# Seven gated sums of an S2-MLP block: from VectorE and GpSimd to GpSimd alone

## The chip, the cores and the metric

The kernel runs on one core of one Trainium2 chip. The core has a matrix engine (TensorE, PE in the profile; its weight loads are PEld), a vector engine (VectorE, DVE), an engine for functions and copies (ScalarE, ACT), a general engine (GpSimd, POOL), and SyncE (SP), which here issues most of the DMAs. Each engine works through its own list of instructions in the order in which the program was written, and waits on semaphores for the others. The metric is the device time of one execution, in microseconds (us); lower is better.

## What is computed

A block with adaptive layer norm: attention with 32 heads over 2048 tokens of width 512, and then a mixer in two halves, each part gated by a row made from the condition c.

```python
h = _layernorm(x, axis=-1) * (1 + ca) + sa
x = x + ga * _A_ref(h, A_wqkv, A_wo)            # attention
h = _layernorm(x, axis=-1) * (1 + cb) + sb
x = x + gb * _B_ref(h, B_w1, B_w2, B_w3, B_w4)  # the mixer

# _B_ref(x):
h = _gelu(_layernorm(x, axis=-1) @ w1)
hs = shifted(h) @ w2          # four quarters of the columns, shifted by +1, -1, +2, -2 rows
x1 = x + hs                   # the mixer's first half
h2 = _gelu(_layernorm(x1, axis=-1) @ w3) @ w4
return x1 + h2
```

Seen from the result, the mixer adds gb * x1 and gb * h2 to x. The change concerns the first of these two sums.

## The kernel before

**Tiles and chunks.** The 2048 rows are 16 tiles of 128 rows (NKT = 16); four tiles are a chunk (TPC = 4, NC = 4). Attention takes the first three quarters of the time. Its softmax works on all engines, and GpSimd prepares the low parts of the probabilities (L1061). What comes after attention is the tail: for every chunk wo, a layer norm, w1 with gelu, the shift and w2, a layer norm, w3 with gelu, and w4. Chunk 0's tail begins while attention still runs.

**Precision.** Each matmul of the tail is three matmuls in a reduced format, of high and low parts (`mm3`, L358 to 364: lines 359, 361 and 363). So each operand is split: ScalarE copies the high part, VectorE or GpSimd subtracts for the low one. For an activation transposed on TensorE that is L353 and L349, both into A; for a gelu's result it is L1459 and, on GpSimd, L1460. Weights of w3 and w4 are split at their first use (`fresh`, L1191): a load to `raw`, for w4 alone a GpSimd multiplication by the gate's row gbrow (L1210), ScalarE's copy (L1211), VectorE's subtraction (L1212), and then a store to Ws in DRAM for later chunks, from which the rings of weights are loaded.

**One tile in the tail.** `tail(ci)` (L1283) is a generator of chunk ci's work up to w2. Here x1 is the tile of x and xb the tile of the mixer. After wo, VectorE adds the result to x1 (`x1_add`, L1406), takes statistics (L370, L371, L1353), GpSimd makes the reciprocal root (`rstd`, L1356), and VectorE writes the modulated norm to xb (`center` L1415, `scale` L1418). A second norm follows: statistics of xb, GpSimd's `shift` (L1356, L1360 and L1361, three operations on the small tile trs), and ScalarE's xn (`ln_apply`, L1367). TensorE transposes xn (L1247), and w1 follows. After w2, VectorE adds its result to xb (`xb_add`, L1511), and the same statistics, shift and xn (L370, L1356, L1367) make w3's input. Then xb holds half of the mixer's first half (gelu's factor of one half is left out on the way), and the list `z` (L1515, L1516) adds it to x1 with the gate: VectorE multiplies xb by 2 and by gbrow, and GpSimd adds xb to x1. `rest(ci)` (L1527) does w3 and w4 and adds w4's result to x1 (`z_add`, L1560); the tile is then stored (L1568).

Chunk 0 takes tiles 0, 1, 2 through w2 (the shift wants the rows after a tile). Chunk 1 takes tiles 3 and 4, then 5 and 6; chunk 2 takes 7 to 10, and chunk 3 takes 11 to 15.

**The order of the work.** `Sched` (L112) plans the order of each engine's instructions while the program is written; nothing is decided on the chip. It keeps a planned time for PE, ACT, DVE and POOL (T["P"], "A", "D", "G"). A generator's matmuls advance PE's time. Operations that follow are put into a chain, a list of (engine, cost, function); the next one is ready 170 ns after the one before (XX). `misc` (L171) picks from the chains the operation for an engine that can start first, and, among equals, the one of the chain that stands first in the list, by its priority (`prio`: 1 for the norms, and 2, the last, for z, ZPRIO at L75) and then by age. It takes an operation only if it fits:

```python
if start + ch[1][0][1] <= until + AGE * max(0.0, self.T[e] - ch[0]) and (not best or start < best[0]):
```

Here start is the later of the engine's time and the time when the operation is ready, ch[1][0][1] is its cost, ch[0] the time when it is ready, and AGE is 0.2. In the tail, `step` (L295) sets the horizon `until` 500 ns beyond the later of the engine's time and PE's time + 100 ns. The costs are `cD` = 602 ns and `cG` = 2.2 x 512 + 40 = 1166 ns for a tile of 512 columns; a `shift` counts 850 ns and a `rstd` 464 (L1364, L1363). The `rstd` of `center` is put into GpSimd's list at once (L1414).

`mark(("z", t))` notes that tile t's sum has been put into the lists. Only then does `rest` put w4's matmuls for that tile (L1554), and `tail(ci)` of chunks 2 and 3 begins its tile t only when tile t - 8 has that mark (L1399).

Of the kernel before, what the change touches and what calls it, by code (L numbers as in the profile page):

```python
# [15 lines left out]
OP = mybir.AluOpType  # L16
# [4 lines left out]
S, D, H, DH, F = 2048, 512, 32, 16, 1792  # L21
# [5 lines left out]
TPC = CH // P  # L27
# [294 lines left out]
def cD(n=CH):  # L322
    return n / 0.96 + 69


def cG(n=CH):
    return 2.2 * n + 40
# [3 lines left out]
def kernel(ctx, tc, A_x, A_wqkv, A_wo, B_w1, B_w2, B_w3, B_w4, c, w_mod, out):  # L331
    nc = tc.nc
    te, act, dve, pool, dma = nc.tensor, nc.scalar, nc.vector, nc.gpsimd, nc.sync
# [21 lines left out]
    def mark(key):  # L355
        return None, 0, lambda: done.add(key)
# [44 lines left out]
    gbrow = con.tile([P, D], F32, name="gbrow")  # L401
# [23 lines left out]
    def dbank(n):  # L425
        return sch.take(lambda i: psd["d"].tile([P, CH], F32, name=n, tag=f"s{i}" if psd["s"] else f"d{i}", bufs=1))
# [308 lines left out]
    for i in range(NV):  # L735
        t = qp.tile([P, H // 4, 192], BF16, name=f"vt{i}")
# [486 lines left out]
    def pool_of(ci):  # L1223
        return fa if ci < NB or (ci - NB) % 2 else tp
# [28 lines left out]
    def spawn(gen, key):  # L1253

        def run():
            yield from gen
            done.add(key)
        sch.add(run(), 0)

    def rows_mm(b, lhs, w, ks, nk):  # L1260

        for k in ks:
            wh, wl = w[k // 2]
            for _ in mm3(b, lhs(k, 0), lhs(k, 1), wh[:, k % 2], wl[:, k % 2], k == 0, k == nk - 1):
                yield nsq(CH)
# [17 lines left out]
    def tail(ci):  # L1283
# [56 lines left out]
        else:  # L1340
            t = oh[0].tile([P, NRAW, CH], F32, name="raw", tag="osb0", bufs=1)
# [3 lines left out]
        def ln_ops(src, mean=False):  # L1345

            st = fa.tile([P, 6], F32, name="tst", tag="tst", bufs=8)
            mv = fa.tile([P, 2], F32, name="tmv", tag="tmv", bufs=10)
            rs = fa.tile([P, 2], F32, name="trs", tag="trs", bufs=10)

            def stats():
                ln_stats(st, mv, src)
                dve.tensor_scalar(mv[:, 1:2], mv[:, 1:2], EPS, None, op0=OP.add)  # L1353

            def rstd():
                pool.tensor_tensor(rs[:, 0:1], mv[:, 1:2], mhalf[:, 0:1], op=OP.pow)  # L1356

            def shift():
                rstd()
                pool.tensor_tensor(rs[:, 1:2], mv[:, 0:1], rs[:, 0:1], op=OP.mult)  # L1360
                pool.tensor_scalar(rs[:, 1:2], rs[:, 1:2], -1.0, 1.0, op0=OP.mult, op1=OP.mult)  # L1361
            if mean:
                return rs, mv, (("D", cD() + 150, stats), ("G", 464, rstd))  # L1363
            return rs, (("D", cD() + 150, stats), ("G", 850, shift))  # L1364
# [10 lines left out]
        def normed(key, t, rs):  # L1375
            tag = xtag(key, t)
            xlive[tag] = xlive.get(tag, 0) + 1
            x = xn[key, t] = (tp if tag == "x4" else fa).tile([P, D], F32, name="xn", tag=tag, bufs=XN[tag])
            y = xbt[t]
            return ln_apply(x, y, rs), mark((key, t))  # L1380
# [6 lines left out]
        def xn_room(key, t):  # L1387
            return xlive.get(xtag(key, t), 0) < XN[xtag(key, t)]

        def norm_T(ts, key, i):  # L1390

            yield lambda: all((key, t) in done for t in ts) and (key == "xn" or not ci or ("w3", ci - 1) in done)
            An[key, i] = A = tA("A4" if key == "xn4" else "A", i, len(ts) * P)
            yield from transposed(lambda k, j: xn[key, ts[j]][:, k * P:(k + 1) * P], range(KT), len(ts), A)
            xlive[xtag(key, ts[0])] -= len(ts)

        for i, t in enumerate(new):
# [4 lines left out]
            x1 = x1t[t]  # L1402
            xb = xbt[t] = pool_of(ci).tile([P, D], F32, name="xb", tag="xb", bufs=XBF if pool_of(ci) is fa else XBT)
# [98 lines left out]
        for si, ts in enumerate(sub):  # L1502
            yield lambda: all(("g", ci, i, n) in done for i in range(1 + (t0 + 1 in ts)) for n in range(4))
            for t in ts:
                yield lambda: sch.room() and xn_room("xn4", t)
                b = dbank("w2")
                yield from rows_mm(b, lambda k, p: g[:, k, p, 130 + (t - t0) * P - SH[k]:][:, :P], w, range(KT), KT)
                xb, x1 = xbt[t], x1t[t]

                def xb_add(xb=xb, b=b):  # L1510
                    dve.tensor_tensor(xb, xb, b, op=OP.add)  # L1511
                    sch.free(b)

                r, ops = ln_ops(xb)
                z = (("D", cD(), lambda xb=xb: dve.scalar_tensor_tensor(xb, xb, 2.0, gbrow, op0=OP.mult, op1=OP.mult)),  # L1515
                     ("G", cG(), lambda xb=xb, x1=x1: pool.tensor_tensor(x1, x1, xb, op=OP.add)), mark(("z", t)))  # L1516
                sch.chain(("D", cD(), xb_add), *ops, *normed("xn4", t, r),
                          (None, 0, lambda z=z: sch.chain(*z, prio=ZPRIO)), bank=b, prio=NPRIO)
            spawn(norm_T(ts, "xn4", si), ("T4", ci, si))
# [82 lines left out]
    for k, blk in enumerate(blocks + [[]] * (LAG + CPER)):  # L1602
# [18 lines left out]
        t, start = CIN, 0.0  # L1621
# [53 lines left out]
        if blk and blk[0] <= 2 * (NS - T0S) <= blk[-1]:  # L1675
            sch.add(tail(0))
# [9 lines left out]
    with ExitStack() as ex:  # L1686
        ep = ex.enter_context(tc.tile_pool(name="ep", bufs=1, space=PSUM))
        psd["d"], psd["s"] = ep, False
        att.close()
        akx.close()  # L1690
        tpx = ExitStack()
        tp = tpx.enter_context(tc.tile_pool(name="tp", bufs=1))
        big["A"] = tp.tile([P, 4 * KT * 2 * P], F32R, name="A")
        big["g2"] = tp.tile([P, 4 * KT * 2 * P], F32R, name="g2")
        done.add("C")
        rings["f"] = Ring(FRONT * (NC - NB), [("wf", BF)] * BF)
        for ci in range(NB, NC):
            sch.add(tail(ci), ci - NB)
        while sch.busy():
            sch.step()  # L1700
        tpx.close()
# [29 lines left out]
```

## Time and profile before

| what | us |
|---|---|
| time, median of 3 runs | 2021.24 |
| lowest and highest | 2019.19, 2022.35 |
| profiled execution | 2021.44 |
| its span, first to last instruction | 2019.7 |
| TensorE busy | 1934.4 |
| VectorE busy | 1656.3 |
| GpSimd busy | 1571.9 |
| ScalarE busy | 1510.2 |

The views shown below are read so. A row of the page names a group of instructions by its line, engine and operation, with out<-in by the program's names. In a stretch of time the columns are the busy times of PE, PEld, DVE, ACT and POOL with the number of instructions in brackets, the granted clock of TensorE as a part of full speed, the busy share of the DMA engines, and GB/s. A list of waits gives engine and line, whom it waited for, the us in total, how often, and the longest. A row of the timeline gives the start and the duration in us, the engine, the line, the operation with its shapes, and in square brackets how long the engine stood idle just before, and who ended that. Merged rows (x2 and more) count several instructions in a row.

### The profile page before, as it was taken

To read this page: it belongs to the slowest core of one execution; us is meant where nothing else is said; L and a number is where in the kernel's file an instruction comes from. 1 tells how busy PE (TensorE), PEld (TensorE's weight loads), DVE (VectorE), ACT (ScalarE), POOL (GpSimd) and SP (SyncE) were. 2 spreads that over 40 slices of the span, in tenths; PEclk is the share of its full clock that TensorE was granted. 3 is DMA by queue.
4 is the path that set the end of the run, shared out by engine and by line. 5 is a ranking of instruction groups with operands and counts; after the bars stand their busy time and mean duration, and the time that the engine had idled before them with its cause. 6 is when DMAs were issued, how large, how long until landed. Compare 5 with 4: busy or idle time off the path is not lost.

```text
span 2019.7 us, 41655 instructions
## 1 busy us (share of the span) xinstructions
PE 1934.4 (96%) x14456; PEld 1162.1 (58%) x14456; DVE 1656.3 (82%) x2979; ACT 1510.2 (75%) x3085; POOL 1571.9 (78%) x1488
## 2 busy tenths in 40 slices
PE   7999999999999999999999999999998999999999
PEld 5755545454444444444444444444455878898998
DVE  6398888879999999999999999999975886556443
ACT  6438987768999999999999999999985544344443
POOL 6349988879999999999999999999996554435222
PEclk9989999999999999999999999999999999999999
DMA  8777675445343434444443435354414676553541
GB/s 295 233 204 192 151 187 155 135 130 124 86 92 87 91 88 83 96 82 97 81 98 75 104 72 107 72 136 126 99 46 158 230 261 265 226 200 116 201 153 68
DMA packets 185508, 278.01 MB, mean 138 GB/s; under 512 B 117104, under 2 KB 127856, under 8 KB 169008
## 3 DMA queue, kind: packets, MB, share of 16 engines
q1 hardware_dynamic: 181792, 267.20, 49.1%
q10 hardware_dynamic: 2304, 4.20, 0.6%
q0 software_dynamic: 1200, 3.93, 0.5%
q8 instruction: 115, 1.88, 0.4%
q14 instruction: 97, 0.79, 0.1%
HBM read 211.81 MB, written 62.91 MB: 136 GB/s over the span
## 4 chain that ended last, share of the span: by engine, by line
PE 61%; DVE 16%; ACT 9%; issue 6%; POOL 4%; DMA 3%; SPq 0%; ACTq 0%; POOLq 0%; DVEq 0%
PE mb L996 13%; DVE mx L992 12%; PE pv L1086 9%; PE sc L1012 8%; ACT pt L1008 7%; PE w L363 5%; PE w L359 5%; PE w L361 5%; PE pv L1083 4%; PE ot L1113 3%; POOL pt L1061 2%; PE xT L1247 1%; POOL trs L1356 1%; PE v L359 1%; DMA wr<-Ws 1%
## 5 line engine op out<-in xcount | busy, mean ns | idle before, releaser
L1061 POOL TENSOR_SCALAR pt<-pt 128x1024 f16<-128x1024 uint16 x953 | 1248.3, 1367 | 79.9 <-ACT pt L1008 76.7
L992 DVE TENSOR_REDUCE mx<-mb 128x1 f32<-128x512 f32 x2048 | 1250.0, 681 | 72.7 <-PE mb L996 63.5
L1008 ACT ACTIVATE pt<-sc 128x512 int32<-128x512 f32 x2048 | 1060.9, 614 | 123.5 <-PE mb L996 97.1
L996 PE MATMUL mb<-kst,qtl 62*128 62x512 f32 x2048 | 781.1, 461 | 20.5 <-ACT pt L1008 10.0
L1012 PE MATMUL sc<-qtl,kst 64*128 64x512 f32 x2048 | 739.3, 449 | 4.6 <-DVE mx L992 1.8
L996 PEld LDWEIGHTS mb<-kst,qtl 62*128 62x128 f32 x2048 | 358.9, 193 | 233.7 <-ACT pt L1008 160.4
L1012 PEld LDWEIGHTS sc<-qtl,kst 64*128 64x128 f32 x2048 | 336.6, 185 | 185.4 <-DVE mx L992 118.7
L1086 PE MATMUL pv<-pt,vst 128*32 128x512 f16 x4096 | 384.8, 397 | 20.6 <-ACT ac L1103 20.6
L1460 POOL TENSOR_TENSOR g<-sq,g 128x256 fp32r<-128x256 f32 (+1 forms) x124 | 96.8, 785 | 188.9 <-ACT g L1459 176.6
L1083 PE MATMUL pv<-pt,vst 128*32 128x512 f16 (+1 forms) x2048 | 220.8, 389 | 2.5 <-POOL pt L1061 2.4
L1086 PEld LDWEIGHTS <-vst 128*32 128x32 bf16 x4096 | 91.8, 93 | 227.2 <-issue 208.8
L361 PE MATMUL w<-A,wr 128*128 128x256 f32 (+1 forms) x520 | 153.4, 295 | 0.3 <-DVE A L349 0.3
L359 PE MATMUL w<-A,wr 128*128 128x256 f32 (+1 forms) x520 | 153.2, 295 | 0.3 <-ACT A L353 0.3
L363 PE MATMUL w<-A,wr 128*128 128x256 f32 (+1 forms) x520 | 153.1, 294 | 0.0
L1456 ACT ACTIVATE sq<-w 128x256 f32<-128x256 f32 (+1 forms) x130 | 52.1, 401 | 127.0 <-PE w L363 117.5
L363 PE MATMUL w<-wr,g 128*128 128x512 f32 x270 | 106.5, 394 | 3.1 <-POOL g L1460 3.1
L359 PE MATMUL w<-wr,g 128*128 128x512 f32 x270 | 106.9, 396 | 1.8 <-DMA wr<-Ws 1.8
L361 PE MATMUL w<-wr,g 128*128 128x512 f32 x270 | 106.1, 393 | 0.0
L1438 DVE SCALAR_TENSOR_TENSOR sq<-sq,w 128x256 f32<-128x256 f32 (+1 forms) x130 | 58.1, 449 | 56.5 <-ACT sq L1458 56.3
L359 PEld LDWEIGHTS w<-A,wr 128*128 128x128 f32 x520 | 98.7, 190 | 1.7 <-ACT A L353 0.5
L361 PEld LDWEIGHTS w<-A,wr 128*128 128x128 f32 x520 | 98.7, 190 | 1.6 <-DVE A L349 0.5
L363 PEld LDWEIGHTS w<-A,wr 128*128 128x128 f32 x520 | 98.6, 190 | 0.5 <-issue 0.5
(156 smaller groups left out, 2131.6 us busy)
## 6 DMA issues: line engine op xcount, KB each, us to landing
wr<-Ws SPq DMA_DIRECT2D x66, 1024.0 KB, 5.2
vst<-Vs SPq DMA_DIRECT2D x64, 768.0 KB, 5.7
kst<-Ks SPq DMA_DIRECT2D x126, 384.0 KB, 6.1
Ws<-wr SPq DMA_DIRECT2D x14, 1024.0 KB, 5.0
qtl<-Qs SPq DMA_DIRECT2D x128, 96.0 KB, 4.3
Vs<-vt SPq DMA_DIRECT2D x32, 384.0 KB, 4.2
Ks<-qk SPq DMA_DIRECT2D x16, 512.0 KB, 3.8
Qs<-qk SPq DMA_DIRECT2D x16, 512.0 KB, 3.0
```

The lines of the kernel that those rows point to most:

```text
L359: te.matmul(o, lh, rh, start=first, stop=False)
L361: te.matmul(o, lh, rl, start=False, stop=False)
L363: te.matmul(o, ll, rh, start=False, stop=last)
L992: end = sch.crit("D", 605, e + PX, lambda: dve.reduce_max(mxs[u][:, j, g, c:c + 1], b, axis=AX.X))
L996: return ready, lambda: te.matmul(b, lhs, kst[u % 3][r, c * CH:(c + 1) * CH], start=True, stop=True), after
L1008: ea = sch.crit("A", 480, e + PX, lambda: act.activation(pt[s][:, j], b, AF.Exp))
L1012: return ready, lambda: te.matmul(b, kst[u % 3][r, kt * P:(kt + 1) * P], qst[u][r], start=True, stop=True), after
L1061: e_low[s] = XP["G"] + sch.crit("G", 1345, ready, lambda: pool.tensor_scalar(o, i, 0.5, 1.0, op0=OP.mult, op1=OP.mult))
L1083: te.matmul(acc[r:r + n, :], v[:, kt + i, c:c + n].bitcast(F16), pt[s + i].bitcast(F16)[:, j, 0::2], start=False, stop=kt == NKT - 2, skip ...
L1086: te.matmul(acc[r:r + 32, :], v[:, kt, r:r + 32], pt[s].bitcast(F16)[:, j, 1::2], start=kt == 0, stop=False, skip_group_check=True)
L1113: te.matmul(b[:, t * n:(t + 1) * n], ac[:, t * P:(t + 1) * P], smat.rearrange("p j d -> p (j d)"), start=True, stop=True)
L1460: ("G", cG(n), lambda: pool.tensor_tensor(lo, sq, hi, op=OP.subtract)), (None, 0, end), bank=b)
```

## The change

For the tiles t below 2 * TPC - 1 = 7, which are those that chunks 0 and 1 take through w2, the two operations of z become one GpSimd step with a planned cost of three times cG. In it GpSimd multiplies xb by gbrow and then adds xb to x1 twice, in place of VectorE's multiplication by 2 and gbrow and GpSimd's one addition. Tiles 7 to 15 keep the list that they had. The mark, the priority and the place of the chain after xn are the same.

```diff
                 r, ops = ln_ops(xb)
-                z = (("D", cD(), lambda xb=xb: dve.scalar_tensor_tensor(xb, xb, 2.0, gbrow, op0=OP.mult, op1=OP.mult)),
+                def z_sum(xb=xb, x1=x1):
+                    pool.tensor_tensor(xb, xb, gbrow, op=OP.mult)
+                    pool.tensor_tensor(x1, x1, xb, op=OP.add)
+                    pool.tensor_tensor(x1, x1, xb, op=OP.add)
+
+                z = (("G", 3 * cG(), z_sum), mark(("z", t))) if t < 2 * TPC - 1 else \
+                    (("D", cD(), lambda xb=xb: dve.scalar_tensor_tensor(xb, xb, 2.0, gbrow, op0=OP.mult, op1=OP.mult)),
                      ("G", cG(), lambda xb=xb, x1=x1: pool.tensor_tensor(x1, x1, xb, op=OP.add)), mark(("z", t)))
                 sch.chain(("D", cD(), xb_add), *ops, *normed("xn4", t, r),
                           (None, 0, lambda z=z: sch.chain(*z, prio=ZPRIO)), bank=b, prio=NPRIO)
```

## The prediction

> **What bounds the kernel now.** I first read the page's busy shares, then the busy time in stretches, to find the stage that holds the changed operations.
>
> ```profile
> span 2019.7 us, 41655 instructions
> PE 1934.4 (96%) x14456; PEld 1162.1 (58%) x14456; DVE 1656.3 (82%) x2979; ACT 1510.2 (75%) x3085; POOL 1571.9 (78%) x1488
> ```
>
> The profiled execution took 2021.44 us: the span and 1.74 us around it. It stands 0.20 us above the median of the three runs, 2021.24. TensorE (PE) is busy 96% of the span, so a change pays or costs only where PE stands still. Next, the two edited lines and three stretches of 40 us around them.
>
> ```profile
> L1515 DVE SCALAR_TENSOR_TENSOR xb<-xb,gbrow x16: 675/682/918, 1558.7 to 1864.8; 128x512 f32<-128x512 f32 x16
> L1516 POOL TENSOR_TENSOR x<-x,xb x16: 1268/1292/1717, 1559.7 to 1865.6; 128x512 f32<-128x512 f32 x16
> ...
> 1560.00:1600.00 40.00, 34.91 (x170) 31.06 (x171) 34.47 (x65) 17.90 (x34) 23.67 (x30) 0.91 0.56 196
> 1600.00:1640.00 40.00, 36.55 (x220) 32.41 (x220) 31.20 (x62) 22.03 (x49) 23.27 (x34) 1.00 0.78 280
> 1640.00:1680.00 40.00, 36.38 (x188) 31.93 (x187) 35.70 (x64) 20.97 (x42) 24.28 (x24) 1.00 0.75 273
> ...
> 1720.00:1760.00 40.00, 40.00 (x229) 34.93 (x229) 25.66 (x55) 14.51 (x34) 18.27 (x29) 1.00 0.56 212
> ```
>
> The columns are PE, weight loads, VectorE (DVE), ScalarE (ACT), GpSimd (POOL), granted clock, DMA share and GB/s. All sixteen gated sums lie between 1558 and 1866 us; the seven that change lie before 1640. There PE loses 12.16 us in 120 (40 minus 34.91, 36.55 and 36.38), while from 1720 to 1760 it loses none. DVE is the fullest helper, 34.47 and 35.70 of 40; POOL has some 16 us free in each stretch. Then I listed what PE waited for from 1540 to 1720, and where.
>
> ```profile
> PE xT L1247 <- ACT xn L1367: 12.6, 7, 2.9
> PE w L363 <- POOL g L1460: 2.2, 1, 2.2
> ...
> 1563.87 2.40 PE L1247 MATMUL xT<-ident,xn 128*128 128x128 f32 x10 [2.94 <-ACT xn L1367]
> 1582.53 0.98 PE L1247 MATMUL xT<-ident,xn 128*128 128x128 f32 x7 [1.54 <-ACT xn L1367]
> 1605.38 0.98 PE L1247 MATMUL xT<-ident,xn 128*128 128x128 f32 x7 [2.52 <-ACT xn L1367]
> 1652.70 0.50 PE L363 MATMUL w<-wr,g 128*128 128x512 f32 x1 [2.23 <-POOL g L1460]
> 1659.21 0.98 PE L1247 MATMUL xT<-ident,xn 128*128 128x128 f32 x7 [1.40 <-ACT xn L1367]
> ```
>
> PE's stalls are waits for layer-normed tiles, and each of these passes through the small POOL operations that make the reciprocal root (trs). So what counts is not POOL's total load but what stands ahead of a trs or a raw scaling (L1210) in POOL's queue, which runs in the order the program was written.
>
> **What the change does to the engines.** For tiles 0 to 6 it removes one DVE operation each, and puts three POOL operations where there was one. A POOL one takes 1.29 us, 1.25 from start to start in a row, so a sum grows from 1.29 to about 3.8 us; 14 added operations are 14 x 1.25 = 17.5 us, against 48.8 us free (three times 40, less 23.67, 23.27 and 24.28). DVE loses 7 x 0.60 = 4.2 us, start to start. POOL has room on average; the terms below are places.
>
> **Where the sums go.** The planner issues a sum only when planned start + cost fits under its horizon: 600 ns beyond PE's planned time (100 + 500) plus a fifth of the wait. The cost rises from 1166 to 3499 ns. So a sum now goes out 2.9 us of PE time after its possible start, less a fifth of its age, where it was 0.57 us; a trs (850 or 464) or a raw scaling (1166) that turns up in between passes it. At an age of (3499 - 500) / 0.2 = 15.0 us it goes out whatever PE does. So the sums move later, as blocks of 3.8 us, among critical small operations. I apply this to the trace's times, which the planner's estimates need not match.
>
> **First stall (tiles 0 to 2).**
>
> ```profile
> 1558.68 0.69 DVE L1515 SCALAR_TENSOR_TENSOR xb<-xb,gbrow 128x512 f32<-128x512 f32 x1 [0.33 <-ACT xn L1367]
> 1559.29 0.68 DVE L1511 TENSOR_TENSOR xb<-xb,w 128x512 f32<-128x512 f32 x1
> 1560.46 2.17 ACT L1211 ACTIVATE wr<-raw 128x512 fp32r<-128x512 f32 x4
> 1563.00 0.81 ACT L1367 ACTIVATE xn<-xb,trs 128x512 f32<-128x512 f32 x1 [0.37 <-POOL trs L1361]
> ```
>
> Tile 0's gate holds up tile 2's sum xb on DVE by 0.33 + 0.61 = 0.94 us. Without it tile 2's trs is ready 0.9 us sooner, but ACT is busy with four weight copies until 1562.63, so its xn gains the 0.37 us of idle time alone: **-0.4 us**, bounds -0.94 (the copies are planned elsewhere) and 0. Tile 0's POOL block, not ready until xn at 1558.65, fits only after tile 2's trs, which it spares.
>
> **Second stall (tiles 4 and 5, chunk 1's first half).**
>
> ```profile
> 1573.17 0.99 POOL L1356 TENSOR_TENSOR trs<-tmv,mhalf 128x1 f32<-128x1 f32 x1 [4.77 <-DVE tmv L1353]
> 1577.23 1.51 POOL L1356 TENSOR_TENSOR trs<-tmv,mhalf 128x1 f32<-128x1 f32 x2 [3.07 <-DVE tmv L1353]
> ```
>
> Tile 0's block runs to about 1566.7, a raw scaling to 1568.0, tile 1's block to 1571.8. Tile 2's sum is by then 8 us old (1571.8 less 1563.81, the end of its xn), needs 2.9 - 1.6 = 1.3 us of PE time beyond 1571.8, and so comes about when the first trs does. Behind it: 1574.2 + 3.75 = 1577.9, and the pair of trs at 1577.23 starts 0.7 us late; ahead of it: 1575.6, which makes the first trs 2.4 us late. Both feed the stall at 1582.53. I take **+0.7 us**, bounds 0 and +2.4. The DVE gates of tiles 1 and 2 go from before 1566; DVE is then idle, waiting for PE, for 3.13 us:
>
> ```profile
> 1570.79 0.69 DVE L1406 TENSOR_TENSOR x<-x,wo 128x512 f32<-128x512 f32 x1 [3.13 <-PE wo L363]
> ```
>
> so they bring nothing; without that wait they would bring 1.2 us. Tile 3's block fits before tile 6's trs at 1632.40 (next fence): POOL idled 2.71 us there, after a sum of 1.29 us that goes, 4.0 us for a block of 3.8: nothing, and up to 2.5 us if it starts that much later. The stall at 1605.38 is set by a load into raw, behind which ACT's queue stands; no sum lies near it.
>
> **Third and fourth stall (tiles 4 to 6).**
>
> ```profile
> 1632.40 0.55 POOL L1356 TENSOR_TENSOR trs<-tmv,mhalf 128x1 f32<-128x1 f32 x1 [2.71 <-DVE tmv L1353]
> 1633.88 0.81 ACT L1367 ACTIVATE xn<-xb,trs 128x512 f32<-128x512 f32 x1 [1.20 <-POOL trs L1361]
> 1637.37 0.68 DVE L1515 SCALAR_TENSOR_TENSOR xb<-xb,gbrow 128x512 f32<-128x512 f32 x1
> 1638.12 1.28 POOL L1516 TENSOR_TENSOR x<-x,xb 128x512 f32<-128x512 f32 x1 [3.03 <-DVE xb L1515]
> 1639.36 1.29 POOL L1210 TENSOR_TENSOR raw<-raw,gbrow 128x512 f32<-128x512 f32 x1
> 1641.35 0.83 DVE L1212 TENSOR_TENSOR wr<-raw,wr 128x512 fp32r<-128x512 f32 x1 [1.10 <-ACT wr L1211]
> 1650.68 0.99 POOL L1356 TENSOR_TENSOR trs<-tmv,mhalf 128x1 f32<-128x1 f32 x1 [6.38 <-DVE tmv L1353]
> 1652.60 1.00 POOL L1356 TENSOR_TENSOR trs<-tmv,mhalf 128x1 f32<-128x1 f32 x1
> 1654.10 2.55 POOL L1210 TENSOR_TENSOR raw<-raw,gbrow 128x512 f32<-128x512 f32 x2
> 1656.62 0.54 POOL L1356 TENSOR_TENSOR trs<-tmv,mhalf 128x1 f32<-128x1 f32 x1
> 1658.36 0.80 ACT L1367 ACTIVATE xn<-xb,trs 128x512 f32<-128x512 f32 x1
> ```
>
> Before, POOL waits 3.03 us for tile 6's gate on DVE, and the raw scaling behind it feeds the DVE operation that waits 1.10 us at 1641.35. After, tile 4's block runs 1633.8 to 1637.6. If the raw scaling follows at once, it is 1639.36 - 1637.6 = 1.8 us earlier, and DVE, freed of two gates (1.2 us), can use it; if tile 5's block comes first, it starts at 1641.4 at the earliest, 2.0 us late. PE's 2.23 us wait at 1652.70 hangs on this stretch of DVE. Bounds -1.8 and +2.0; I take **0**, as the two orders are about as likely.
>
> Tile 6's sum is ready at 1634.7 and by its age goes out at about 1649.7, when POOL's queue already holds the trs of chunk 2's first tile. So it stands behind the group at 1652.60, ahead of the raw scalings at 1654.10 and the trs at 1656.62, and all behind it is late by 3 x 1.29 = 3.9 us: that trs, the xn at 1658.36, and PE's transposes at 1659.21. The late raw scalings also hold up the copy of w4's weights on ACT and DVE, the release of raw's buffers, and through them SyncE's queue (loads of raw, stores to Ws, ring loads), all by the same 3.9 us at most. I take **+3.9 us**; bounds 0 (the block fits in the 6 us that POOL stands idle before 1650.68, or PE is given other matmuls first) and +3.9.
>
> **The interface between DVE and POOL.**
>
> ```profile
> L1212 DVE TENSOR_TENSOR wr<-raw,wr x28: 678/686/1780, 1561.6 to 1673.7; 128x512 fp32r<-128x512 f32 x28
> L1212 DVE TENSOR_TENSOR wr<-raw,wr 128x512 fp32r<-128x512 f32 x28 | 25.8, 943 | 1.3 <-ACT wr L1211 1.3
> ```
>
> DVE's subtraction of weights has two inputs in SBUF. It takes 0.68 us at best, 0.94 on average and 1.78 at worst, with POOL active beside it. At the average excess, 14 added POOL operations cost DVE 14 x 0.265 = 3.7 us, about what it saves (4.2): nothing on the path. The Trainium skill (SBUF — State Buffer, "The single rule") says that a DVE instruction with two SBUF inputs and a GpSimd operation lock the shared ports for a whole instruction, and the second is blocked until the first ends. By that rule the added POOL time would be DVE's loss wherever they meet, up to 14 x 1.25 = 17.5 us as an estimate; the trace shows a lesser loss on average (0.27 us a subtraction).
>
> **Sum.** -0.4 + 0.7 + 0 + 3.9 + 0 = +4.2 us on 2021.44 us: 2025.6 us.
>
> **Rivals.**
> *Faster: DVE's relief reaches PE.* For it speaks that DVE is busy 35.70 of 40 us and that the 2.23 us stall stands at the end of a DVE chain with a gate's wait in it; 1.8 us of it can go. The first stall also has a price beyond its length, in the granted clock (seventh column):
>
> ```profile
> 1563.00:1564.00 1.00, 0.13 (x1) 0.13 (x2) 1.00 (x2) 0.81 (x1) 1.00 (x1) 0.51 0.73 84
> ...
> 1569.00:1570.00 1.00, 1.00 (x4) 0.77 (x3) 0.00 (x0) 0.07 (x1) 0.00 (x0) 0.58 0.75 178
> 1570.00:1571.00 1.00, 1.00 (x6) 0.82 (x5) 0.21 (x1) 0.00 (x0) 0.00 (x0) 1.00 0.97 365
> ```
>
> From 1563.9 to about 1569.8 PE runs at half its clock, and loses half of 5.9 us, 3.0 us, which the stall of 2.52 us at 1605.38 did not bring. If the first stall falls from 2.94 to that by its 0.4 us, and tile 6's block lies in POOL's idle time before 1650.68, the kernel gains 0.4 + 3.0 + 1.8 = 5.2 us: 2016.2 us. It decides from the point where tile 6's block begins by 1650.68 - 3.8 = 1646.9. Against it: the age rule sends that sum later, and 0.4 us is a thin margin.
>
> *Slower by more: a second stretch at half clock.* The same delay makes the stall at 1659.21 1.40 + 3.9 = 5.3 us long, longer than the 2.94 us that came with the slow clock. The same price again gives 4.2 + 3.0 = +7.2 us: 2028.6 us. Against it: the planner counts the block too and may put matmuls before the transposes. The Trainium skill (TensorE: Matmul & The Clock Gate, "Part 1: The HAM clock gate") puts the fall to half rate after one idle window of about 3.4 us that runs freely; a stall of 5.3 us would contain a whole one in (5.3 - 3.4) / 3.4, some 6 cases of 10, as an estimate. The slow stretch in the trace agrees with it in depth (0.51 at its start).
>
> *No difference: PE is given other work.* The planner writes PE's order as well, so its view of a late xn moves matmuls of w3 and w4 ahead of the transposes. Then the 3.9 us vanish: 2021.44 - 0.4 + 0.7 = 2021.7 us. Against it: those matmuls want weights whose raw scalings stand behind the same block.
>
> *The sum itself is awaited.* w4's matmuls for a tile are planned only after its sum.
>
> ```profile
> 1594.88 1.88 DVE L1560 TENSOR_TENSOR x<-x,w 128x512 f32<-128x512 f32 x3
> ```
>
> Their first results are added at 1594.88, 17 us after tile 2's sum would end (1577.9). I give this no chance of its own. That the change leaves DVE's gates in place can't be: both lists of operations are written out, and one is chosen by the tile's number.
>
> **How the numbers follow.** Forecast 0.40 (own range 2022.5 to 2028.5); faster 0.30; slower by more 0.17; no difference 0.13. The range 2014.5 to 2031.5 goes down to the faster case with the fourth stall's 1.40 us gone as well (2014.8), and up to half of the 6 us between 2028.6 and the sum of the upper bounds left out there (1.7 more at the second stall, 2.0 at the third, 2.5 for tile 3). A measurement of this kernel can tell about 0.2%, or 4.04 us: 2017.2 to 2025.3. Of the forecast's 0.40, 0.28 lies above that and 0.12 within; with the rival above, slower is 0.45. Same is 0.12 + 0.13 + 0.02 of the faster case, which may gain less than 4 us: 0.27. Faster is 0.28.
>
> **What would show it.** In the changed trace POOL has 21 operations of about 1.25 us on the new lines for tiles 0 to 6, in blocks of three, and DVE nine gates, all after 1700 us. The first step is right if the stall near 1563.9 is 2.5 us; the second if a trs near 1577 starts behind a block; the fourth if a block stands ahead of the last trs before the transposes near 1659 and PE waits there 3 us or more. If that wait is 1.4 us or less, the step on tile 6 is wrong, and with it the forecast. If L1212's mean rises from 0.943 towards 1.2 us, the interface costs what I set at nothing. A stall anywhere after 1720, or another order of PE's tiles, would be an effect that this working does not have.

## The result and the profile after

The changed kernel takes 2037.25 us in the median of 4 runs (2034.30 to 2037.96), the kernel before 2020.54 us beside it (4 runs). The ratio is 1.0082, with a 95% interval from 1.0067 to 1.0097: 16.7 us slower. The profiled execution took 2037.32 us, its span 2034.9, 15.2 more than the span before.

The busy shares of the page after the change:

```profile
span 2034.9 us, 41659 instructions
PE 1942.9 (95%) x14456; PEld 1169.8 (57%) x14456; DVE 1652.1 (81%) x2972; ACT 1510.6 (74%) x3085; POOL 1589.2 (78%) x1502
```

The lists hold what the change says: seven instructions fewer on DVE, 14 more on POOL. PE runs as many matmuls as before but is busy 8.5 us longer, and idle 92.0 us (2034.9 - 1942.9), 6.7 more. What happens ahead of the sums nearly cancels out, so the two executions are compared from the first of PE's waits beside the sums to the end, first after, then before:

```profile
1557.55:2034.90 477.35, 445.17 (x2581) 397.79 (x2580) 279.37 (x556) 199.88 (x460) 212.34 (x286) 0.97 0.51 183
```

```profile
1558.14:2019.70 461.56, 438.78 (x2581) 393.20 (x2580) 282.30 (x565) 199.69 (x460) 194.94 (x272) 0.99 0.52 190
```

In these rows stand the length of a stretch, the busy time of PE, its weight loads, DVE, ACT and POOL with their instructions, the granted clock, the DMA share and GB/s. With the same 2581 matmuls the stretch is 15.8 us longer: PE is busy 6.4 us more, and idle 9.4 us more (32.18 for 22.78). The stretches around the seven sums, after the change:

```profile
1520.00:1560.00 40.00, 35.19 (x226) 27.66 (x224) 20.15 (x44) 20.32 (x46) 19.05 (x32) 0.91 0.51 184
1560.00:1600.00 40.00, 32.81 (x150) 29.10 (x151) 32.22 (x58) 18.12 (x35) 31.75 (x36) 0.87 0.59 210
1600.00:1640.00 40.00, 35.44 (x202) 31.03 (x201) 24.06 (x52) 17.75 (x41) 15.70 (x27) 0.91 0.60 213
1640.00:1680.00 40.00, 30.29 (x145) 26.09 (x144) 30.23 (x54) 19.03 (x36) 37.48 (x36) 0.83 0.60 222
1680.00:1720.00 40.00, 40.00 (x242) 36.21 (x241) 28.14 (x53) 15.26 (x36) 16.65 (x23) 1.00 0.82 298
```

Two columns tell the story. POOL is busy 37.48 of 40 us between 1640 and 1680, where it had 24.28; and the granted clock, which was 1.00 there, is 0.83, with 0.87 and 0.91 in the two stretches before. (The 0.91 of the first row comes from 1535 to 1545 us, at 0.69 and 0.62; that lies ahead of the first sum and isn't the change's.) PE's longer stalls in order of time:

```profile
1562.41 2.39 PE L1247 MATMUL xT<-ident,xn 128*128 128x128 f32 x10 [2.46 <-ACT xn L1367]
1587.62 1.30 PE L1247 MATMUL xT<-ident,xn 128*128 128x128 f32 x7 [4.77 <-ACT xn L1367]
1611.65 0.98 PE L1247 MATMUL xT<-ident,xn 128*128 128x128 f32 x7 [0.22 <-ACT xn L1367]
1627.36 0.79 PE L359 MATMUL w<-wr,g 128*128 128x512 f32 x1 [4.32 <-DMA wr<-Ws]
1668.00 0.80 PE L363 MATMUL w<-wr,g 128*128 128x512 f32 x1 [3.29 <-POOL g L1460]
1675.43 1.75 PE L1247 MATMUL xT<-ident,xn 128*128 128x128 f32 x7 [6.42 <-ACT xn L1367]
```

Against the stalls before they are -0.48, +3.23, -2.30, +3.38, +1.06 and +5.02 us: 9.9 us of waiting. (The fourth was 0.94 us; its row comes with the experiment on that load.) The 6.4 us of slower matmuls are the clock. A finer view, 5 us wide, shows stretches at half clock at the first stall, which had one before the change as well, and around the 6.42 us one:

```profile
1560.00:1565.00 5.00, 2.59 (x11) 2.53 (x12) 4.79 (x7) 3.99 (x9) 4.68 (x6) 0.58 0.64 229
...
1670.00:1675.00 5.00, 0.00 (x0) 0.00 (x0) 2.83 (x6) 2.78 (x6) 4.76 (x7) 0.50 0.37 115
1675.00:1680.00 5.00, 4.57 (x15) 3.89 (x16) 2.11 (x3) 2.92 (x6) 5.00 (x6) 0.50 0.00 0
```

Where the sums now stand in POOL's queue is best seen in its timeline. Around the second stall and the last ones, with some rows between left out:

```profile
1571.69 1.00 POOL L1356 TENSOR_TENSOR trs<-tmv,mhalf 128x1 f32<-128x1 f32 x1
1572.66 1.29 POOL L1210 TENSOR_TENSOR raw<-raw,gbrow 128x512 f32<-128x512 f32 x1
...
1577.94 0.98 POOL L1356 TENSOR_TENSOR trs<-tmv,mhalf 128x1 f32<-128x1 f32 x1 [0.77 <-DVE tmv L1353]
1578.90 1.29 POOL L1516 TENSOR_TENSOR xb<-xb,gbrow 128x512 f32<-128x512 f32 x1
...
1584.22 1.59 POOL L1356 TENSOR_TENSOR trs<-tmv,mhalf 128x1 f32<-128x1 f32 x2 [0.97 <-DVE tmv L1353]
...
1652.66 1.28 POOL L1516 TENSOR_TENSOR xb<-xb,gbrow 128x512 f32<-128x512 f32 x1
1657.32 0.54 POOL L1356 TENSOR_TENSOR trs<-tmv,mhalf 128x1 f32<-128x1 f32 x1
1657.83 1.28 POOL L1210 TENSOR_TENSOR raw<-raw,gbrow 128x512 f32<-128x512 f32 x1
1659.08 1.74 POOL L1516 TENSOR_TENSOR xb<-xb,gbrow 128x512 f32<-128x512 f32 x1
1664.02 2.06 POOL L1356 TENSOR_TENSOR trs<-tmv,mhalf 128x1 f32<-128x1 f32 x2
...
1667.91 1.26 POOL L1516 TENSOR_TENSOR xb<-xb,gbrow 128x512 f32<-128x512 f32 x1
1671.83 1.26 POOL L1210 TENSOR_TENSOR raw<-raw,gbrow 128x512 f32<-128x512 f32 x1
1673.05 0.55 POOL L1356 TENSOR_TENSOR trs<-tmv,mhalf 128x1 f32<-128x1 f32 x1
```

Each row of L1516 opens a block of three operations, 4 to 5 us long. Tile 3's begins at 1645.52. From 1652.66 on three more, of tiles 4 to 6, alternate with weight scalings and reciprocal roots, and POOL hardly waits for anybody: what was a queue of small answers has become a backlog. The last root, at 1673.05, releases the xn that ends the 6.42 us stall.

In DVE's timeline two rows of scale (L1418) stand out; it takes 0.74 us when nothing disturbs it:

```profile
1572.81 1.70 DVE L1418 SCALAR_TENSOR_TENSOR xb<-xb,trs,sbrow 128x512 f32<-128x512 f32 x1
1578.96 1.77 DVE L1418 SCALAR_TENSOR_TENSOR xb<-xb,trs,sbrow 128x512 f32<-128x512 f32 x1
```

Both begin just after POOL has ended the root that scale waits for and has begun its next operation (1572.66, 1578.90).

### The profile page after: what moved, and what is told of

Its sections match the earlier page's. It is cut to its first block, busy times and chain, and to the rows that moved or that the text cites. A ratio compares the mean times of both kernels' runs of the same rounds, so it can differ in the third digit from the quotient of the medians.

```text
span 2034.9 us, 41659 instructions
## 1 busy us (share of the span) xinstructions
PE 1942.9 (95%) x14456; PEld 1169.8 (57%) x14456; DVE 1652.1 (81%) x2972; ACT 1510.6 (74%) x3085; POOL 1589.2 (78%) x1502
## 4 chain that ended last, share of the span: by engine, by line
PE 62%; DVE 15%; ACT 10%; issue 5%; POOL 4%; DMA 2%; SPq 1%; ACTq 0%; POOLq 0%; DVEq 0%
PE mb L996 13%; DVE mx L992 11%; PE pv L1086 10%; PE sc L1012 8%; ACT pt L1008 7%; PE w L359 5%; PE w L363 5%; PE w L361 5%; PE pv L1083 4%; PE ot L1113 3%; POOL pt L1061 2%; PE xT L1247 1%; DMA wr<-Ws 1%; PE v L359 1%; POOL trs L1356 1%
## 5 line engine op out<-in xcount | busy, mean ns | idle before, releaser
L363 PE MATMUL w<-A,wr 128*128 128x256 f32 (+1 forms) x520 | 153.8, 296 | 0.0
L359 PE MATMUL w<-wr,g 128*128 128x512 f32 x270 | 109.5, 406 | 5.1 <-DMA wr<-Ws 5.1
L363 PE MATMUL w<-wr,g 128*128 128x512 f32 x270 | 108.6, 402 | 4.2 <-POOL g L1460 4.2
L361 PE MATMUL w<-wr,g 128*128 128x512 f32 x270 | 108.1, 400 | 0.0
L363 PEld LDWEIGHTS w<-A,wr 128*128 128x128 f32 x520 | 99.4, 191 | 0.6 <-issue 0.5
```

Source lines behind the costliest of these rows:

```text
L359: te.matmul(o, lh, rh, start=first, stop=False)
L361: te.matmul(o, lh, rl, start=False, stop=False)
L363: te.matmul(o, ll, rh, start=False, stop=last)
```

## The experiments

Three theories were set against each other. ORDER: the planned cost of 3499 ns spoils the order on all engines. LOAD: 14 more POOL operations cost time wherever they stand. PLACE: they cost it only where roots and weight scalings queue behind them. Each edit is shown against the changed kernel.

**Order and load apart.** Four kernels on one chip; the kernel before took 2020.42 us there (13 runs). The first keeps the order of before and runs the new operations:

```diff
-                z = (("G", 3 * cG(), z_sum), mark(("z", t))) if t < 2 * TPC - 1 else \
+                z = (("D", cD(), lambda: None), ("G", cG(), z_sum), mark(("z", t))) if t < 2 * TPC - 1 else \
```

> Planned with the costs of before (a vector-engine step of 602 ns that writes no instruction, then a GpSimd step of 1166 ns), so that every list keeps its order of before; the seven sums run the three GpSimd operations of the change. Theory ORDER (the planned cost of 3499 ns puts the sums as late blocks ahead of the reciprocal roots, and that is the loss): 2020 to 2025 us. Theory LOAD (14 more GpSimd operations and their lock against the vector engine are the loss, wherever they stand): 2032 to 2042 us, and scale (L1418) well above its 0.87 us mean.

Measured: 2032.97 us, ratio 1.0059 [1.0044, 1.0074]. LOAD's range holds the time, ORDER's ends 8 us below it. The trace has the matmuls in the order of before, and POOL's list too but for the added operations. But LOAD's sign fails: scale's mean stays at 0.870 us (0.869 before), and L1212's at 0.957 (0.943). The time goes in POOL's queue. The longest stalls of this kernel:

```profile
1566.58 2.40 PE L1247 MATMUL xT<-ident,xn 128*128 128x128 f32 x10 [5.72 <-ACT xn L1367]
...
1661.33 0.80 PE L363 MATMUL w<-wr,g 128*128 128x512 f32 x1 [4.99 <-POOL g L1460]
```

The first is 2.8 us longer than before: tile 0's block, in the place of its one addition, stands ahead of tile 2's root. The second was 2.23 us.

The second kernel keeps the order of the change and runs one addition a sum, without the gate:

```diff
                 def z_sum(xb=xb, x1=x1):
-                    pool.tensor_tensor(xb, xb, gbrow, op=OP.mult)
-                    pool.tensor_tensor(x1, x1, xb, op=OP.add)
                     pool.tensor_tensor(x1, x1, xb, op=OP.add)
```

> The plan of the change (one step of 3499 ns, the same order on every engine), but each of the seven sums is one GpSimd addition: the gate's multiplication and the second addition are left out. Theory ORDER: 2031 to 2037 us, most of the 16.7 us stays. Theory LOAD: 2016 to 2023 us.

Measured: 2031.69 us, ratio 1.0054 [1.0039, 1.0069]. ORDER's range holds it: with no POOL operation more than before, two thirds of the loss are there. Three of the change's four new stalls appear in it:

```profile
1586.23 1.67 PE L1247 MATMUL xT<-ident,xn 128*128 128x128 f32 x7 [4.46 <-ACT xn L1367]
...
1625.55 0.79 PE L359 MATMUL w<-wr,g 128*128 128x512 f32 x1 [4.12 <-DMA wr<-Ws]
...
1670.48 1.76 PE L1247 MATMUL xT<-ident,xn 128*128 128x128 f32 x7 [5.39 <-ACT xn L1367]
```

The third has both edits, so that the seven gates are gone from DVE and nothing else is changed.

> The plan of before, one GpSimd addition a sum as before, and no gate on the vector engine for the seven tiles (the gate is left out): the change's relief alone. My forecast counted it at -0.4 us, with up to 5.2 us if it reaches TensorE. Theory ORDER and theory LOAD both expect 2015 to 2021 us.

Measured: 2020.00 us (10 runs), ratio 0.9995 [0.9985, 1.0006]. The relief of 4.2 us on DVE is worth nothing that the time can tell (the interval goes from 3.0 us faster to 1.2 us slower), even where POOL pays nothing for it. It does reach PE's waits: in this trace the first stall is 2.46 us, and of the 2.23 us before PE's L363 0.4 are left.

So order alone costs about 11 us, load alone about 12, and both together 16.7: less than their sum. That fits with stalls they share (a late root ends one stall, whatever made it late), but no run shows it stall by stall.

The fourth kernel plans the three operations one by one:

```diff
-                z = (("G", 3 * cG(), z_sum), mark(("z", t))) if t < 2 * TPC - 1 else \
+                z = (("G", cG(), z_a), ("G", cG(), z_b), ("G", cG(), z_b), mark(("z", t))) if t < 2 * TPC - 1 else \
```

Here z_a is the multiplication and z_b one addition.

> The same three GpSimd operations, planned as three steps of 1166 ns each, so that the planner may put a reciprocal root or a weight scaling between them. Theory ORDER: a large part of the loss goes, 2020 to 2028 us. Theory LOAD: no better than the change, 2033 to 2040 us.

Measured: 2037.64 us, ratio 1.0082 [1.0067, 1.0097]: no better than the change, as LOAD had it and against ORDER. Small pieces fit earlier, and so they stand ahead of more roots: its stalls before 1570 are 3.69 and 4.83 us, and its longest, 9.54 us, ends at 1677.

**Which cost in the plan.** One addition a sum again, but planned at 1166 ns:

```diff
-                z = (("G", 3 * cG(), z_sum), mark(("z", t))) if t < 2 * TPC - 1 else \
+                z = (("G", cG(), z_sum), mark(("z", t))) if t < 2 * TPC - 1 else \
```

> One GpSimd addition a sum and no gate (the gate is left out), planned as one GpSimd step of 1166 ns where the change plans 3499; the vector engine's step is gone from the plan too. If the planned cost of 3499 ns spoils the order, this is near the kernel before: 2017 to 2023 us, against 2031.7 with the cost of 3499. If any other order than the one of before costs as much, 2027 to 2035 us.

Measured: 2023.45 us (10 runs), ratio 1.0010 [0.9999, 1.0022], beside 2021.45 us before. Between this kernel and the one of 2031.69 us only the number 3499 differs. Some 9 us of the order's cost come from it (1.0054 to 1.0010); a change of the order as such, which this kernel has too, costs 2 us by this ratio, whose interval reaches down to nothing.

**Which tiles.** Three kernels with another condition on the tile's number, on the same chip as the last one:

```diff
-                z = (("G", 3 * cG(), z_sum), mark(("z", t))) if t < 2 * TPC - 1 else \
+                z = (("G", 3 * cG(), z_sum), mark(("z", t))) if t >= 2 * TPC - 1 else \
```

> The change turned round: the nine tiles 7 to 15 take the new step, with 27 GpSimd operations for 18, and tiles 0 to 6 keep the old list. There GpSimd and the vector engine have room (11 to 21 us and 17 to 26 us busy of 40) and the weights are not split any more. Theory PLACE (the operations cost only where reciprocal roots and weight scalings queue behind them): 2018 to 2024 us. Theory LOAD (each moved sum costs about 16.7 / 7 = 2.4 us): 2042 us.

Measured: 2023.31 us (10 runs), ratio 1.0011 [1.0001, 1.0021]. Nine sums here cost about 2 us, seven in the changed kernel 16.7. So it is not LOAD but the place. What makes the place is less clear than PLACE had it, for small roots queue behind blocks here too, as in this stretch of POOL's timeline:

```profile
1743.07 1.62 POOL L1518 TENSOR_TENSOR x<-x,xb 128x512 f32<-128x512 f32 x1
1744.65 0.55 POOL L1356 TENSOR_TENSOR trs<-tmv,mhalf 128x1 f32<-128x1 f32 x1
```

Yet PE is busy 20.00 of 20 us from 1740 to 1760, as before. It has other work to hand there, and no weights are split any more; no run tells these two apart.

With `t < TPC - 1`, chunk 0's three tiles alone:

> The new step for tiles 0 to 2 alone, with its planned cost. If the loss is one of each place, chunk 0's share is the stall near 1587 and, if the ring load's delay comes from chunk 0's sums too, the stall near 1627: 2026 to 2031 us. If chunk 1's sums make the late loads, 2022 to 2025 us.

Measured: 2030.81 us, ratio 1.0056 [1.0037, 1.0076]. Both stalls are there, 4.96 us at 1585.90 and 4.29 us for the ring load at 1625.50, so three sums near 1570 bring a stall at a load 55 us later.

With `TPC - 1 <= t < 2 * TPC - 1`, chunk 1's four tiles alone:

> The new step for tiles 3 to 6 alone. The two stalls near 1668 and 1675 of the changed kernel (9.7 us against 3.6 before, and a slower clock behind them) belong to these tiles: 2027 to 2031 us, with no stall over 3 us before 1640.

Measured: 2033.94 us, ratio 1.0062 [1.0043, 1.0081]. No new stall before 1640, as expected, and behind it a single one of 9.77 us:

```profile
1662.14 0.79 PE L363 MATMUL w<-wr,g 128*128 128x512 f32 x1 [9.77 <-POOL g L1460]
```

Two stalls of the changed kernel have become one of the same total (3.29 + 6.42 = 9.71 us). The time is above the range expected; why is not shown. The two halves cost 0.56% and 0.62%, together more than the whole.

**The same sums, later.** Chunk 1's tiles with the new step, held back in the plan:

```diff
-                          (None, 0, lambda z=z: sch.chain(*z, prio=ZPRIO)), bank=b, prio=NPRIO)
+                          (None, 0, lambda z=z, t=t: sch.chain(*z, prio=ZPRIO, ready=sch.now() + 45000.0 if TPC - 1 <= t < 2 * TPC - 1 else None)), bank=b, prio=NPRIO)
```

> The new step for tiles 3 to 6 alone, with the same three GpSimd operations and planned cost, but not ready in the plan until 45 us after xn, when the weights are split. Theory PLACE: 2018 to 2024 us, against 2033.9 without the delay. Theory LOAD: 2030 to 2036 us.

Measured: 2028.36 us (10 runs, 2021.30 to 2033.99), ratio 1.0028 [1.0013, 1.0042]. About half of the loss of 0.62% goes; the time lies between the two theories' ranges, and PLACE had expected all of the loss to go. The blocks now run from 1679.70 to 1701.1, and the next roots stand behind them: the stall there is 5.29 us, where it was 2.04 us before.

```profile
1699.38 1.75 POOL L1518 TENSOR_TENSOR x<-x,xb 128x512 f32<-128x512 f32 x1
...
1702.49 0.56 POOL L1356 TENSOR_TENSOR trs<-tmv,mhalf 128x1 f32<-128x1 f32 x1
...
1714.56 1.75 PE L1247 MATMUL xT<-ident,xn 128*128 128x128 f32 x7 [5.29 <-ACT xn L1367]
```

**The slow ring load.** From the chain of waits, first after, then before, with PE's wait of before under it:

```profile
1618.82 8.50 DMA wr<-Ws
```

```profile
1612.66 5.12 DMA wr<-Ws
1617.82 0.50 PE L359 MATMUL w<-wr,g 128*128 128x512 f32 x1 [0.94 <-DMA wr<-Ws]
```

My theory was that this load of w2's weights stands in SyncE's queue behind loads and stores that wait for late weight scalings. The test gives it another queue (w2's loads go to ScalarE's):

```diff
-                    sch.dma(dma.dma_start, w.bitcast(F32), Ws[i])
+                    sch.dma((act if pieces[i][0] == "w2" else dma).dma_start, w.bitcast(F32), Ws[i])
```

> The changed kernel, with w2's two ring loads issued by the scalar engine in place of SyncE; the other lists keep their order. If the stall near 1627 (4.32 us, and a slower clock behind it) comes from that load's place in SyncE's queue behind loads of raw and stores to Ws that wait for late weight scalings, it goes: at most 1.5 us of wait there, and 2031 to 2034 us. If the load is late for its own buffer or for the DMA engines' bandwidth, the stall stays at 3 us or more and the time at 2036 to 2039 us.

Measured: 2038.22 us, ratio 1.0072 [1.0056, 1.0089]; the stall is 5.29 us. The theory falls. From issue to landing the load took 9.0 us on the other queue. It is the transfer that is slow: 8.50 us for the 5.12 before explains the whole growth of the stall (3.38 us). In both traces PE comes to wait 4.22 us after the issue. Over the load's own time the 16 DMA engines are fully busy (1.04) in the changed kernel:

```profile
1618.82:1627.32 8.50, 4.22 (x30) 3.62 (x28) 3.09 (x8) 3.96 (x12) 3.45 (x5) 0.90 1.04 404
```

Before, the share over the load's time was 0.86:

```profile
1612.66:1617.78 5.12, 4.22 (x30) 3.62 (x28) 3.71 (x9) 3.62 (x11) 2.10 (x4) 1.00 0.86 308
```

SyncE's own timeline shows what precedes the load in the changed kernel, five issues in the five microseconds ahead of it, where two stood before:

```profile
1614.08 0.33 SPq L135 DMA_DIRECT2D Ws<-wr  x1
1614.51 1.33 SPq L135 DMA_DIRECT2D raw<-in_B_w_dram  x2
1615.89 1.10 SPq L135 DMA_DIRECT2D Ws<-wr  x1
1617.04 0.49 SPq L135 DMA_DIRECT2D raw<-in_B_w_dram  x1
1618.82 3.20 SPq L135 DMA_DIRECT2D wr<-Ws  x2
```

So the new order bunches the weight traffic just ahead of this load. That the bunch is what slows it is read from these rows; no run took the bunch away.

The control, the same edit in the kernel before:

> The same two loads on the scalar engine's queue in the kernel before, as a control: there TensorE waits only 0.94 us for them. 2018 to 2023 us.

Measured: 2023.10 us (10 runs), ratio 1.0009 [0.9999, 1.0020]. No gain there either; the stall, 0.94 us before, was 3.04 us in its profile.

**The lock.** In the kernel with the new order and one addition, the addition is replaced by an operation that reads nothing:

```diff
-                    pool.tensor_tensor(x1, x1, xb, op=OP.add)
+                    pool.memset(xb, 0.0)
```

> As the run with the plan of the change and one addition, but in place of the addition GpSimd sets xb to zero after its last reader, an operation that reads nothing from SBUF (the gated sum is left out). If scale's 1.78 us near 1577 (0.74 alone) is a lock between a vector operation with two SBUF inputs and a GpSimd operation that reads SBUF, scale falls to 0.7 to 0.8 us there, while the other one near 1571, beside a weight scaling, stays near 1.7 us. If it waits for something else, both stay.

The seven sums are left out here. One run, 2029.04 us. The two scales in it, and PE's stall behind them:

```profile
1570.04 1.70 DVE L1418 SCALAR_TENSOR_TENSOR xb<-xb,trs,sbrow 128x512 f32<-128x512 f32 x1
1576.20 0.75 DVE L1418 SCALAR_TENSOR_TENSOR xb<-xb,trs,sbrow 128x512 f32<-128x512 f32 x1
...
1583.84 0.98 PE L1247 MATMUL xT<-ident,xn 128*128 128x128 f32 x7 [3.43 <-ACT xn L1367]
```

The second fell from 1.78 to 0.75 us, the first, beside the weight scaling, stayed. The memset, too, began just ahead of scale, at 1576.12, and took 0.53 us; scale ran beside it and did not wait for its end. The stall behind fell from 4.46 to 3.43 us, by the same 1.03. So it behaves as a lock against an operation that reads SBUF, and there it lies on PE's path.

## Why the prediction was wrong

The direction was right, and so was the kind of cost (blocks ahead of roots in POOL's queue); the size was not: +4.2 us forecast, 16.7 measured, above the range.

- *First stall, -0.4.* Right, and by the path named: 2.46 us for 2.94, -0.48, and ACT's xn follows the weight copies without the 0.37 us of idle time.
- *Second stall, +0.7.* Wrong, +3.23. I let the sums move within the order that I had and asked only how long a root waits for a block. The planner made another order. Tile 2's block landed behind tile 5's root, not tile 4's, and there its own 3.8 us are not the cost: with one addition in its place the stall is 4.46 us of the 4.77. What costs is that POOL starts its next operation as soon as it has released scale, which then waits about 1 us at the lock, twice, and that tile 5's last root came in a pair behind tile 6's first (the row at 1584.22). The run with the memset shows 1.03 us for one of the locks; the other lock and the pair are read from the chain that ends in this stall, and no run took them away.
- *The interface, 0.* Wrong where it matters. I priced it by L1212's average excess of 0.27 us over the added operations. L1212's mean in fact fell, from 0.943 to 0.884 us; scale's rose, three of its eight operations meeting a POOL operation that began just after POOL had released them:

```profile
L1212 DVE TENSOR_TENSOR wr<-raw,wr 128x512 fp32r<-128x512 f32 x28 | 23.9, 884 | 3.5 <-ACT wr L1211 3.5
L1418 DVE SCALAR_TENSOR_TENSOR xb<-xb,trs,sbrow 128x512 f32<-128x512 f32 x8 | 9.6, 1194 | 1.6 <-POOL trs L1356 1.6
```

  Scale averaged 869 ns before. The rule of the Trainium skill that I had cited (SBUF — State Buffer, "The single rule") describes the two cases at the second stall: the second to start waits for the first one's whole operation. An average over instructions that mostly do not meet POOL hid that.
- *The ring load.* I had no term for it; it is +3.38 us, and -2.30 us came at the stall near 1605, where PE was given other work first, as one rival had it for the fourth. The prediction bounded all effects on the weight traffic by the 3.9 us of tile 6's block. The run with chunk 0's sums alone has this stall (4.29 us) without that block.
- *Third and fourth stall, 0 and +3.9.* Tile 6's block does stand ahead of a weight scaling and the last root; the size was short: +1.06 and +5.02. A block took 4.0 to 5.0 us, not 3.8, and tiles 3 to 5, which I placed earlier (tile 3 before 1632.40), went out from 1645.52 on, into the same stretch.
- *The clock.* A rival, at 0.17 and 3.0 us. It became the largest term: 6.4 us, beside four stalls of 3.3 to 6.4 us. The Trainium skill (TensorE: Matmul & The Clock Gate, "Part 1: The HAM clock gate") has the half rate follow an idle window of about 3.4 us; the rows agree for the 4.32 and 6.42 us stalls (0.57 from 1625 to 1630 us, 0.50 from 1670 to 1680). My threshold between 2.52 and 2.94 us did not hold: the first stall is 2.46 us after the change and still comes with a clock of 0.58 from 1560 to 1565, so its length alone doesn't decide (two shorter waits precede it).
- *Faster: DVE's relief reaches PE.* Right on one wait, not on the time: without the gates and with nothing added 1.8 of the 2.23 us go, as this rival had it, but the ratio is 0.9995, and its interval excludes a gain of 5.2 us. DVE's 35.70 of 40 us of busy time did not mean that it set PE's pace.

In short, the step that failed is "where the sums go": I applied the planner's rule to seven operations, and left the rest of the order as the trace showed it. The planned cost of 3499 ns changed the rest: in the two traces the matmuls have the same order up to the second stall, and another from there to about 1665. That alone costs about 11 us, with one addition a sum. In the sum of the prediction the miss shows as +0.7 at the second stall (measured 3.23), no term for the ring load (3.38 less 2.30 at the stall near 1605), +3.9 at the fourth (5.02), and nothing for the clock (6.4).

## What to carry to other kernels

Where a planner writes the order, a declared cost is an edit of every engine's list: to see what the operations themselves cost, first keep the old costs and run the new work under them. Before moving work off a busy engine, delete it there and change nothing else; here that run shows no gain that the time can tell, and at most 3.0 us, so in that order no receiver could have won more. An engine that is half idle but answers small requests on the critical path has little room for blocks, since its idle time keeps the answers short; the nine later sums cost little, where PE had other work.

## What the runs showed of the hardware

Scale with two inputs in SBUF took 1.70 to 1.78 us instead of 0.74 when a POOL operation of 128x512 with two inputs in SBUF had begun up to 0.15 us before it, and 0.75 us beside a POOL memset that reads nothing. A GpSimd memset of 128x512 took 0.53 us, a two-input operation of that size 1.28.

```profile
1576.12 0.53 POOL L1516 MEMSET xb<- 128x512 f32 x1
```

Stalls of PE cost more than their length: 9.4 us more of idle time from the first wait on came with 6.4 us of slower matmuls.
